# A decode layer's result as two rows of 320 in two PSUM banks, where it was four rows of 160 in one

## The chip, the cores and the metric

One core of one Trainium2 chip runs the kernel. The metric is the device time of one execution in microseconds (us), as the median of several runs. The engines are named as in the profile: PE is TensorE's matmuls, PEld its weight loads, DVE is VectorE, ACT is ScalarE, POOL is GpSimd, SP is SyncE, which here only issues transfers (DMA).

## The reference

One token (a row x of 640 values, bf16) goes through one layer: attention over a cache of 4096 positions with 32 heads, then a gated feed-forward part. Each part has a layer norm ahead of it and a residual sum behind it.

```
h   = x + attention(layernorm(x), K, V, wq) @ wo
n   = layernorm(h)
out = h + (gelu(n @ w_gate) * (n @ w_up)) @ w_down      # w_down: 1728 x 640
```

The change touches only the last line: the sum of h and the down projection, and how its 640 values leave PSUM.

## The kernel before, in words

The kernel is written instruction by instruction. `Prog` keeps one list for each engine in the order in which the program names the operations; each operation names those it waits for, and semaphores are made from that. An engine works through its own list in order, so an instruction that waits holds up all that is behind it on its engine. All large transfers are issued by SP, in one queue.

K and V of four heads at a time (4 MB) come into three slots in turn. For K, VectorE multiplies by the query (L273), TensorE sums by matmuls with the identity (L281), VectorE reduces (L288) and ScalarE takes the exponential (L292). For V, TensorE multiplies (L310). The query projection ahead of this (L259) is worked in sets of four matmuls of 512 columns, one on each quarter of the output partitions (from 0, 32, 64 and 96), with the sets alternating between PSUM banks 3 and 7. VectorE and ScalarE copy the two banks (L263, L264).

The end of the kernel, in TensorE's order:

- `proj_part` (L348) multiplies by wo. VectorE adds x (L404), which gives h with its values spread over partitions (`hT`, 128 x 5). Then come the layer norm and `hX` (L407), a 128 x 640 tile with each value of h on the diagonal.
- `glu(ps_g, ...)` (L417): the gate projection, 70 matmuls of one output column each.
- `resid` (L424 to L428): matmuls of a column of ones with `hX` put the values of h as a row on one partition in PSUM. They begin the accumulation (`start=True`) onto which the down projection adds. Both operands are fp32.
- `glu(ps_u, ...)` (L430, L431): the up projection, 70 more matmuls of line L417, in two parts, as its weights come in two transfers.
- VectorE and ScalarE work out the gelu of the gate (L432 to L439) beside this. L440 multiplies by the up projection: `hm`, 128 x 14 in bf16, one column for each block m of 128 rows of w_down.
- `hp` and `h2` (L451, L453) prepare the last, half-filled block (m = 13) so that its 64 rows lie over all 128 partitions.
- `down` (L442 to L450): for each block m, a matmul with one column of `hm` as the stationary operand and 640 columns of w_down as the moving one, in pieces. The order of the blocks follows the transfers: 12, then 0 to 3, 13, 4 to 7, 8 to 10, and 11 last, with a wait for the transfer ahead of each group. Block 11 has an operation of its own for each piece, so that each copy waits for its own piece.
- The copies (L460 on VectorE, L462 on ScalarE) bring the pieces from PSUM into `out_row` (1 x 640, bf16); SP then issues the output transfer.

Before the change a block has four pieces of 160 columns. They go to the partitions 0, 32, 64 and 96 of bank 3 (`ps_d`, L151), VectorE copies the first two and ScalarE the last two:

```
ps_d = bank[3][:, 256:416]
i = e.matmul(ps_d[32 * q:32 * q + 1, 0:160], h, wd_sb[:, m, n:n + 160],
             start=False, stop=(m == 11))
```

Bank 7, which the change uses as well, holds half of the query projection and later the wo projection (`ps_p`), which L404 has read by then.

Of the kernel before, what the change touches and what calls it, by code (L numbers as in the profile page):

```python
# [101 lines left out]
def bass_sequential_preLN__gqa_block_cached__glu_gated_geglu__decode_kernel(nc, A_x, A_k_cache, A_v_cache, A_wq, A_wo, B_x, B_w_gate, B_w_up, B_w_down, out):  # L102
# [11 lines left out]
    out_row = sb("out_row", [1, D], BF16)  # L114
# [4 lines left out]
    hX = sb("hX", [128, 128, 5], FP32)  # L119
# [13 lines left out]
    hm = sb("hm", [128, 14], BF16)  # L133
    hm2 = sb("hm2", [128, 2], BF16)
# [4 lines left out]
    ones_f = sb("ones_f", [128, 128], FP32)  # L139
# [6 lines left out]
    bank = [nc.alloc_psum_tensor("bank%d" % i, [128, 512], FP32) for i in range(8)]  # L146
# [1 line left out]
    ps_g, ps_u = bank[0], bank[1]  # L148
    ps_q = [bank[3], bank[7]]
    ps_a = bank[3]  # L150
    ps_d = bank[3][:, 256:416]  # L151
    ps_o = [bank[2], bank[4]]
    ps_s = bank[5]
    ps_z = bank[6]
# [6 lines left out]
    V = lambda fn, *d: P.op("vector", fn, *d)  # L161
    A = lambda fn, *d: P.op("scalar", fn, *d)
    T = lambda fn, *d: P.op("tensor", fn, *d)
# [199 lines left out]
    for kind, G in order:  # L363
# [7 lines left out]
        if G == 4:  # L371
# [15 lines left out]
    wd_sb = sl[1][:, 0:14 * D].rearrange("p (m n) -> p m n", m=14)  # L387
# [3 lines left out]
    d_wd = [P.dma("sync", wd_sb[:, 12, :], B_w_down[1536:1664, :], free[1]),  # L391
            P.dma("sync", wd_sb[:, 13, 0:320], B_w_down[1664:1728, :].rearrange("f (s n) -> (f s) n", s=2))]
# [11 lines left out]
    h = V(lambda e: e.tensor_add(hT[:, 0:5], xx[:, 0:5], ps_p[:, 0:5]), pr)  # L404
# [17 lines left out]


    def resid(e):  # L424
        for q in range(4):
            i = e.matmul(ps_d[32 * q:32 * q + 1, 0:160], ones_f[:, 0:1],
                         hX[:, 32 * q:32 * q + 32, :].rearrange("p a c -> p (a c)"), start=True, stop=False)
        return i  # L428
    T(resid, hx)
    T(glu(ps_u, wu_sb, range(3)), d_wu[0])  # L430
    up = T(glu(ps_u, wu_sb, range(3, 5)), d_wu[1])  # L431
# [7 lines left out]
    g6 = V(lambda e: e.tensor_mul(gu[:, :], g_t[:, :], t1[:, :]), g8)  # L439
    g9 = V(lambda e: e.tensor_mul(hm[:, :], gu[:, :], ps_u[:, 0:14]), g6, up)  # L440

    def down(ms, qs=range(4)):  # L442
        def fn(e):
            for m in ms:
                for q in qs:
                    h, n = (hm[:, m:m + 1], 160 * q) if m < 13 else (hm2[:, q // 2:q // 2 + 1], 160 * (q % 2))
                    i = e.matmul(ps_d[32 * q:32 * q + 1, 0:160], h, wd_sb[:, m, n:n + 160],  # L447
                                 start=False, stop=(m == 11))
            return i
        return fn  # L450
    hp = T(lambda e: e.matmul(ps_z[:, 0:1], sel2[:, :, :].rearrange("p a b -> p (a b)"), hm[0:64, 13:14],  # L451
                              start=True, stop=True), g9, c_sel2)
    h2 = V(lambda e: e.tensor_mul(hm2[:, :], par[:, :], ps_z[:, 0:1].to_broadcast([128, 2])), hp)  # L453
    T(down([12]), d_wd[0])
    T(down(range(4)), d_wd[2])
    T(down([13]), h2, d_wd[1])
    T(down(range(4, 8)), d_wd[3])
    T(down(range(8, 11)), d_wd[4])
    dn = {q: T(down([11], [q]), d_wd[5]) for q in (0, 2, 1, 3)}
    os = [V(lambda e, q=q: e.tensor_copy(out_row[0:1, 160 * q:160 * q + 160], ps_d[32 * q:32 * q + 1, 0:160]), dn[q])  # L460
          for q in range(2)]
    os += [A(lambda e, q=q: e.copy(out_row[0:1, 160 * q:160 * q + 160], ps_d[32 * q:32 * q + 1, 0:160]), dn[q])  # L462
           for q in range(2, 4)]
    d_out = P.dma("sync", out[0, :, :], out_row[:, :], *os)
    P.op("sync", None, d_out)

# [29 lines left out]
```

## Time and profile before

| what | value |
| --- | --- |
| time, median of 3 runs | 203.16 us (203.05 to 203.16) |
| profiled execution, span from the first to the last instruction (its whole time is not given apart) | 201.9 us |
| PE busy in the span | 120.4 us, 60% |
| DVE busy | 101.2 us, 50% |
| ACT busy | 61.1 us, 30% |
| read from HBM | 84.23 MB, 417 GB/s over the span |
| share of the chain that ended last: DMA, PE, DVE | 64%, 16%, 14% |
| mean granted TensorE clock, whole span | 0.825 |
| granted TensorE clock, from about 177 us on | 0.50 |
| L447 (down), PE | 56 matmuls of 128x160, mean 328 ns |
| L426 (resid), PE | 8 records of 128x160 fp32, mean 450 ns |
| L460 on DVE, L462 on ACT | 2 copies of 1x160 each, mean 314 and 286 ns |

How to read it: the profile is one execution, taken by the hardware. A busy share is an average over stages with different limits, so for a change at the end of the kernel the last microseconds are what counts: the chain of work that ended last, and the timeline from about 190 us on. In a timeline row stand the start, the length, the engine, the line, the operation with its output and input and how many there are; brackets give the idle time of the engine before it, and what ended it.

### The profile page before, as it was taken

The numbers are of one execution on the slowest core, as the hardware profiler recorded it, in microseconds if no ns is written. First come the engines' busy times: TensorE is split into PE (matmuls) and PEld (weight loads), VectorE is DVE, ScalarE is ACT, GpSimd is POOL, SyncE is SP. The second block draws the span as 40 slices with busy tenths as digits, with TensorE's granted clock in tenths as the row PEclk, the third lists the DMA queues.
The fourth block names the chain that finished last, engine by engine and source line by source line (L and its number), as shares of the span: only waits on it lengthen the run. The fifth ranks groups of instructions, "written<-read, shape, count | busy, mean of one in ns | idle before, by whom it ended". The sixth has DMA issues, their size and how long they took to land.

```text
span 201.9 us, 2505 instructions
## 1 busy us (share of the span) xinstructions
PE 120.4 (60%) x1010; PEld 58.8 (29%) x1010; DVE 101.2 (50%) x106; ACT 61.1 (30%) x273; POOL 5.0 (2%) x14
## 2 busy tenths in 40 slices
PE   0107058537937668690968197727844887467395
PEld 0103023112312233150324032312331344267383
DVE  3201088517979847924791578277708760100221
ACT  2101004620563550670156125603640363100101
POOL 7200000000000000000000000000000000000000
PEclk9999657995799996997599859988995799955555
DMA  9999999999999999999999999999999999999992
GB/s 357 414 404 467 428 415 416 422 448 458 430 415 422 415 445 448 435 424 416 422 435 441 438 435 424 416 428 441 448 419 435 399 425 437 419 408 435 412 409 113
DMA packets 4335, 84.39 MB, mean 418 GB/s; under 512 B 482, under 2 KB 868, under 8 KB 1508
## 3 DMA queue, kind: packets, MB, share of 16 engines
q1 hardware_dynamic: 4322, 84.23, 97.8%
q8 instruction: 8, 0.13, 0.3%
q14 instruction: 3, 0.02, 0.0%
q10 hardware_dynamic: 2, 0.00, 0.0%
HBM read 84.23 MB, written 0.00 MB: 417 GB/s over the span
## 4 chain that ended last, share of the span: by engine, by line
DMA 64%; PE 16%; DVE 14%; issue 3%; SPq 2%
DMA slot<-in_A_k_cache_dram 42%; DVE prod L273 12%; DMA slot<-in_B_w_down_dram 11%; DMA slot<-in_A_v_cache_dram 11%; PE bank L281 11%; PE bank L310 3%; SPq L51 2%; DVE sc L288 2%; PE bank L319 1%; PE bank L447 0%; DVE out_row L460 0%; PE bank L330 0%; DVE RT L329 0%
## 5 line engine op out<-in xcount | busy, mean ns | idle before, releaser
L281 PE MATMUL bank<-prod,id_b 128*128 128x512 bf16 x256 | 75.4, 454 | 50.8 <-DVE prod L273 50.8
L273 DVE TENSOR_TENSOR prod<-slot,qb 128x4096 bf16<-128x4096 bf16 x32 | 72.4, 2285 | 31.1 <-DMA slot<-in_A_k_cache_dram 31.1
L292 ACT ACTIVATE p_bd<-sc,zero_t 32x32 bf16<-32x32 f32 x128 | 46.4, 362 | 86.3 <-DVE sc L288 85.1
L281 PEld LDWEIGHTS bank<-prod,id_b 128*128 128x128 bf16 x256 | 26.9, 113 | 99.4 <-DVE prod L273 63.1
L288 DVE TENSOR_REDUCE sc<-bank 128x32 f32<-128x512 f32 x32 | 22.0, 688 | 21.4 <-PE bank L281 21.4
L292 ACT ACTIVATION_READ_ACCUMULATOR p_bd<-sc,zero_t 32x1 f32 x128 | 23.5, 184 | 0.0
L310 PE MATMUL bank<-slot,p_bd 128*16 128x512 bf16 x256 | 17.3, 379 | 3.1 <-ACT p_bd L292 2.5
L310 PEld LDWEIGHTS bank<-slot,p_bd 128*16 128x16 bf16 x256 | 9.4, 89 | 7.3 <-ACT p_bd L292 3.0
L319 PE MATMUL bank<-po_sb,hs 128*16 128x128 f32 x64 | 8.4, 274 | 1.1 <-ACT po_sb L314 1.1
L348 PE MATMUL bank<-aP,arena 128*128 128x1 bf16 x160 | 6.7, 178 | 3.8 <-DMA arena<-in_A_wo_dram 3.8
L417 PE MATMUL bank<-hlnT,slot 128*128 128x1 bf16 (+1 forms) x140 | 6.7, 176 | 3.2 <-DMA slot<-in_B_w_gate_dram 3.2
L259 PE MATMUL bank<-arena,xlnB 128*32 128x512 bf16 x40 | 3.9, 565 | 7.2 <-DMA arena<-in_A_wq_dram 7.2
L348 PEld LDWEIGHTS bank<-aP,arena 128*128 128x128 bf16 x160 | 6.6, 131 | 3.9 <-DMA arena<-in_A_wo_dram 2.5
L314 ACT COPY po_sb<-bank 128x512 f32<-128x512 f32 x8 | 4.7, 585 | 9.6 <-PE bank L310 9.6
L417 PEld LDWEIGHTS bank<-hlnT,slot 128*128 128x128 bf16 (+1 forms) x140 | 6.3, 118 | 4.1 <-DVE hX L407 3.3
L319 PEld LDWEIGHTS bank<-po_sb,hs 128*16 128x16 f32 x64 | 5.5, 96 | 4.5 <-issue 2.1
L244 ACT ACTIVATE ln<-ln,eps_t 128x1 f32<-128x1 f32 x2 | 0.6, 294 | 20.3 <-DVE ln L242 20.3
L263 DVE CAST qb<-bank 128x512 bf16<-128x512 f32 x1 | 0.7, 692 | 9.6 <-PE bank L259 9.6
L404 DVE TENSOR_TENSOR hT<-xx,bank 128x5 f32<-128x5 f32 x1 | 0.2, 163 | 10.2 <-PE bank L348 10.2
L233 PE MATMUL bank<-one_bf,x_row 1*128 1x1 bf16 x5 | 0.4, 177 | 6.9 <-DMA x_row<-in_A_x_dram 6.9
L259 PEld LDWEIGHTS bank<-arena,xlnB 128*32 128x32 bf16 x40 | 1.6, 136 | 9.1 <-issue 9.0
L334 DVE TENSOR_SCALAR aT<-bank,rz 16x128 bf16<-16x128 f32 x2 | 0.7, 339 | 6.0 <-PE bank L319 6.0
(65 smaller groups left out, 26.3 us busy)
## 6 DMA issues: line engine op xcount, KB each, us to landing
slot<-in_A_k_cache_dram SPq DMA_DIRECT2D x8, 4096.0 KB, 21.4
slot<-in_A_v_cache_dram SPq DMA_DIRECT2D x7, 4096.0 KB, 17.5
arena<-in_A_wq_dram SPq DMA_DIRECT2D x1, 5120.0 KB, 15.4
slot<-in_A_v_cache_dram SPq DMA_DIRECT2D x2, 2048.0 KB, 20.0
arena<-in_A_wo_dram SPq DMA_DIRECT2D x1, 2560.0 KB, 27.3
slot<-in_B_w_gate_dram SPq DMA_DIRECT2D x1, 2160.0 KB, 16.3
arena<-in_A_wo_dram SPq DMA_DIRECT2D x1, 1920.0 KB, 31.5
slot<-in_B_w_up_dram SPq DMA_DIRECT2D x1, 1296.0 KB, 18.4
```

The lines of the kernel that those rows point to most:

```text
L51: ev = self.op(eng, lambda e: e.dma_start(out, in_), *deps, dma=True)
L259: i = e.matmul(ps_q[hf][32 * j:32 * j + 32, :], xlnB[:, c, :], wq_j[:, c, j, 4 * hf:4 * hf + 4, :], start=(c == 0), stop=(c == 4))
L263: qa = V(lambda e: e.tensor_copy(qb[:, 0:4, :].rearrange("p g d -> p (g d)"), ps_q[0][:, :]), qd)
L273: m = V(lambda e: e.tensor_tensor(out=prod[:, s % 4, :, :], in0=kt[:, 32 * u:32 * u + 32, :], in1=qb[:, G, :].unsqueeze(1).to_broadcast([1 ...
L281: i = e.matmul(ps_f[s % 2][:, :], id_b[:, :], prod[:, s % 4, :, 16 * b:16 * b + 16], start=(b == 0), stop=(b == 7))
L288: reds[s] = V(lambda e: e.reduce_sum(sc[:, s % 4, :], ps_f[s % 2][:, :].rearrange("p (g d) -> p g d", d=16), axis=AX.X), folds[s], exps.ge ...
L292: x = A(lambda e, j=j: e.activation(p_bd[32 * j:32 * j + 32, G % 2, 32 * (s % 4):32 * (s % 4) + 32, j], sc[32 * j:32 * j + 32, s % 4, :], ...
L310: i = e.matmul(po[a:a + 16, :], p_bd[:, G % 2, 4 * b:4 * b + 4, :].rearrange("p g j -> p (g j)"), vt[:, 4 * b:4 * b + 4, :], start=(b < 4) ...
L314: evs[G] = A(lambda e: e.copy(po_sb[:, G % 2, :], po[:, :]), pvs[G], hds.get(G - 2))
L319: i = e.matmul(ps_a[0:16, 128 * (G // 4):128 * (G // 4) + 128], hs[:, r, 12 - 4 * g:28 - 4 * g], po_sb[:, G % 2, 128 * r:128 * r + 128], s ...
L348: r = e.matmul(ps_p[:, c:c + 1], wo_sb[:, t, i, c::5], aP[:, t, i:i + 1], start=(t == 0 and c == 0 and i == 0), stop=(t == 1 and i == 15), ...
L417: i = e.matmul(ps[0:128 if m < 13 else 64, m:m + 1], ws, hlnT[:, c:c + 1], start=(c == 0 and m == 0), stop=(c == 4), skip_group_check=True)
```

## The change

The result is kept as two rows of 320 instead of four of 160: one on partition 0 of bank 3, one on partition 32 of bank 7. The residual becomes two matmuls of 320 columns, the down projection 28 of 320 where it was 56 of 160. Each engine makes one copy of 320 where it made two of 160. Nothing else is changed: the transfers, the order of the blocks and the waits of TensorE stay.

```diff
-    ps_d = bank[3][:, 256:416]
+    ps_d = [bank[3][0:1, 0:320], bank[7][32:33, 0:320]]
...
     def resid(e):
-        for q in range(4):
-            i = e.matmul(ps_d[32 * q:32 * q + 1, 0:160], ones_f[:, 0:1],
-                         hX[:, 32 * q:32 * q + 32, :].rearrange("p a c -> p (a c)"), start=True, stop=False)
+        for q in range(2):
+            i = e.matmul(ps_d[q], ones_f[:, 0:1], hX[:, 64 * q:64 * q + 64, :].rearrange("p a c -> p (a c)"),
+                         start=True, stop=False)
         return i
...
-    def down(ms, qs=range(4)):
+    def down(ms, qs=range(2)):
         def fn(e):
             for m in ms:
                 for q in qs:
-                    h, n = (hm[:, m:m + 1], 160 * q) if m < 13 else (hm2[:, q // 2:q // 2 + 1], 160 * (q % 2))
-                    i = e.matmul(ps_d[32 * q:32 * q + 1, 0:160], h, wd_sb[:, m, n:n + 160],
-                                 start=False, stop=(m == 11))
+                    h, n = (hm[:, m:m + 1], 320 * q) if m < 13 else (hm2[:, q:q + 1], 0)
+                    i = e.matmul(ps_d[q], h, wd_sb[:, m, n:n + 320], start=False, stop=(m == 11))
             return i
...
-    dn = {q: T(down([11], [q]), d_wd[5]) for q in (0, 2, 1, 3)}
-    os = [V(lambda e, q=q: e.tensor_copy(out_row[0:1, 160 * q:160 * q + 160], ps_d[32 * q:32 * q + 1, 0:160]), dn[q])
-          for q in range(2)]
-    os += [A(lambda e, q=q: e.copy(out_row[0:1, 160 * q:160 * q + 160], ps_d[32 * q:32 * q + 1, 0:160]), dn[q])
-           for q in range(2, 4)]
+    dn = [T(down([11], [q]), d_wd[5]) for q in range(2)]
+    os = [V(lambda e: e.tensor_copy(out_row[0:1, 0:320], ps_d[0]), dn[0]),
+          A(lambda e: e.copy(out_row[0:1, 320:640], ps_d[1]), dn[1])]
```

## The prediction

> **What bounds the kernel now.** I read the page's chain of work first, then the chain from 150 us on, piece by piece, because the change touches only the end of the kernel. Its last pieces are:
>
> ```profile
> 176.80 22.42 DMA slot<-in_B_w_down_dram
> 199.22 0.04 issue
> 199.27 0.75 PE bank L447 x16
> 200.02 0.30 DVE out_row L460
> 200.32 0.03 issue
> 200.35 0.32 DVE out_row L460
> ```
>
> The columns are start, length and what it is. Up to 199.22 us the end is set by the weights of the down projection landing. Behind that stand only 0.75 us of matmuls and two copies of VectorE. Second, the timeline of the last 9 us shows what happens beside that transfer (start, length, what; in brackets the idle time before, and what ended it):
>
> ```profile
> 193.12 0.71 PE L426 MATMUL bank<-hX,ones_f 128*1 128x160 f32 x8
> ...
> 193.77 3.36 PE L417 MATMUL bank<-hlnT,slot 128*128 128x1 bf16 x70
> ...
> 197.24 0.17 DVE L440 TENSOR_TENSOR hm<-gu,bank 128x14 bf16<-128x14 f32 x1 [2.17 <-PE bank L417]
> ...
> 197.57 1.50 PE L447 MATMUL bank<-slot,hm 128*1 128x160 bf16 x40
> ...
> 199.27 0.71 PE L447 MATMUL bank<-slot,hm 128*1 128x160 bf16 x16 [0.19 <-DMA slot<-in_B_w_down_dram]
> 199.67 0.09 PEld L447 LDWEIGHTS bank<-slot,hm 128*1 128x1 bf16 x4 [0.18 <-DMA slot<-in_B_w_down_dram]
> 200.01 0.66 DVE L460 CAST out_row<-bank 1x160 bf16<-1x160 f32 x2 [2.17 <-PE bank L447]
> 200.04 0.59 ACT L462 CAST out_row<-bank 1x160 bf16<-1x160 f32 x2 [5.67 <-PE bank L447]
> 200.72 0.31 SPq L51 DMA_DIRECT2D out_dram<-out_row  x1
> ```
>
> What to see: from 193.12 on TensorE works through one queue almost without a gap: the residual (L426), the up projection (L417), ten rows of the down projection (forty matmuls, L447). Then it waits a moment for the last two transfers. So the transfer is the bound by a small margin, and TensorE is right behind it. The margin: a lone L447 matmul lasts 290 ns (the shortest in the view of line L447). With 160 columns at 0.83 ns (below) that is 0.13 us of streaming and 0.16 us until it is done. The forty are therefore streamed by 197.57 + 1.50 - 0.16 = 198.91, and the next could start 0.36 us before it does at 199.27.
>
> **What one matmul costs TensorE.** Line L447 has 56 matmuls of 328 ns on average, 18 us if they ran in turn; they are done in 1.50 + 0.71 us, so four run side by side, one on each quarter of the output partitions (0, 32, 64, 96). Ten fours take 1.50 - 0.16 = 1.34 us, 0.134 us for a four of 160 columns, or 0.83 ns per column. The query projection gives the same rate with other shapes. Its fours have 512 columns and alternate between banks 3 and 7, and their weight loads come every 0.43 us, again 0.83 ns per column (the page prints a clock near full for those first slices, but the spacing is that of the halved clock, twice what L281 has at 1.0, see rival A):
>
> ```profile
> 16.80 0.18 PEld L259 LDWEIGHTS bank<-arena,xlnB 128*32 128x32 bf16 x4 [0.24 <-issue]
> 17.22 0.18 PEld L259 LDWEIGHTS bank<-arena,xlnB 128*32 128x32 bf16 x4 [0.24 <-issue]
> 17.65 0.18 PEld L259 LDWEIGHTS bank<-arena,xlnB 128*32 128x32 bf16 x4 [0.24 <-issue]
> ```
>
> So a set of matmuls side by side costs the columns of one of them, however many lie beside it. That decides the case. The change halves the number of matmuls but doubles the columns of each, and only two quarters are in use instead of four. A row m of the down projection, now one set of 160 columns (0.133 us), becomes one set of 320 (0.267 us).
>
> **The sum, part by part.**
>
> 1. The residual (L426). The view shows eight records for four matmuls: an fp32 matmul passes twice, at 0.27 us a pass. It streams for 0.71 - 0.16 = 0.55 us. Two side by side with 320 columns need twice that: +0.53 us. It hides behind nothing: it stands in TensorE's queue ahead of the up projection, whose weights have landed (the view of transfers gives 20.0 us for the later part, issued at 174.91, so 194.9; it is needed about 195.8), and hm (L440) waits for the up projection, while the gate's part of it is ready at 195.06 (L439). So hm and all behind it slip by 0.53: the first L447 starts at 198.10.
> 2. The down projection. Fourteen sets of 0.267 are 3.73 us, and 0.16 until the last is done: 198.10 + 3.73 + 0.16 = 201.99. The last two transfers (waits ended at 199.27 and 199.67) are in by the time TensorE needs rows 8 and 11, at 200.77 and 201.57, so these waits go; what is late in their place is TensorE itself. Now its last matmul ends at 199.27 + 0.71 = 199.98: +2.01 us. Half the LDWEIGHTS (28 for 56) save nothing, as they lie beside the matmuls.
> 3. The copies. VectorE starts 0.03 after TensorE's end, ScalarE 0.06. Each now copies 160 elements twice, 0.66 and 0.59 us. No row has 320 in one partition, so by the rows on either side: VectorE takes 314 ns for 160 (L460) and 692 for 512 (L263), 1.07 ns more per element, so 314 + 172 = 486; ScalarE 286 (L462) and 585 (L264), so 286 + 136 = 422. The bounds are 314 (length costs nothing) and 632 (nothing but length). I take 486, as 1x160 lies on the same line as 128x14 (173 ns, L432). VectorE ends at 202.02 + 0.49 = 202.51, ScalarE at 202.05 + 0.42 = 202.47; now the end is 200.67. So the copies give back 0.17, and the end moves by +1.84. That the rows lie in two banks gains nothing that I can see: both engines read bank 3 at once today and both first and second copies take the same time (311 to 316, 285 to 286 ns).
> 4. The output transfer (L51) and the end of the program follow the later copy, as now. No transfer ahead of it is moved, and no queue but TensorE's gets longer work.
>
> Span 201.9 + 1.84 = 203.7. The profiled execution's own time is not given apart; the runs' median lies 1.26 above its span, and I add the difference to the median: 203.16 + 1.84 = **205.0 us**. About 0.2% (0.4 us) is what a measurement of this kernel can tell from no change.
>
> **Rivals.**
>
> *A, not slower: the clock opens in time.* The granted clock is 0.50 in every stretch from 177 us to the end. At 1.0 a column costs half: L281's eight matmuls of 512 take 1.90 us, less 0.16, which is 0.42 ns per column. Then a pair of 320 streams in 0.133 us, as a four does now; residual and ten rows end as before, TensorE waits for the transfers again, and what is left is the copies' -0.17: 203.0 us. To come out within 0.4 us of before, TensorE may slip by 0.58 us instead of 2.01, so 1.43 must be saved; as an open clock halves what is left to stream, it must open by 201.83 - 2.86 = 198.97. Against it speaks the view of windows, cut into stretches of 3.41 us, by which the clock's changes are spaced (length, TensorE busy, count, clock):
>
> ```profile
> 28.98:32.39 3.41, 3.41 (x9) 0.50 1.02 442
> 46.04:49.46 3.42, 2.53 (x6) 0.50 1.05 450
> ...
> 192.82:196.23 3.41, 3.41 (x72) 0.50 1.02 412
> ```
>
> After the first, full of 512-column matmuls, the clock was 1.0; after the second, filled to 74%, it was not; nor after the third, which is full, but mostly of 1-column matmuls. A stretch that ends by 198.97 would be nearly all L417. The Trainium skill, "TensorE: Matmul & The Clock Gate", section "What's actually happening", has the clock open after one busy window of some 3.4 us; by that rule, TensorE being in work from 189.85 on, the clock would be open well before the down projection and the result this rival's 203.0. The trace does not agree: 0.50 after a window that was 3.41 of 3.41 busy. Chance 3%.
>
> *B, the clock opens late.* A stretch that is over 75% full of L447 (74% was too little above) ends no earlier than 200.7. In the profile's phase the stretches end at 199.65 and 203.06, so none does; if the phase varies, one of them may fall between 200.7 and 201.8 and save half of what is left, up to 0.6 us: 204.4 to 204.95. A row of one column may also not count as work at all. Chance 12%.
>
> *C, the two rows do not run side by side*, because they lie in different banks. Then the residual streams 2.13 us (+1.6) and the down projection 28 x 0.267 = 7.47: the end of TensorE is 199.17 + 7.47 + 0.16 = 206.80, +6.82, less 0.17: 209.8 us. The fours of L259 keep their pace across a change of bank at each step, which speaks against it, though inside a four they share one. Chance 5%.
>
> **How the numbers follow.** The forecast has 80% (A 3, B 12, C 5). Its own spread is the copies' bounds (-0.17, +0.15) and some tenths for the slack between TensorE and the landings: 204.7 to 205.4. With B the range is 204.4 to 205.4. Slower by over 0.2%: forecast, B and C, 0.96 (1 point off for what I do not see); within 0.2%: A, 0.03; faster: 0.01.
>
> **What would show it.** Right: L447 x28 in one unbroken run of about 3.9 us, no wait for B_w_down before L447, L426 about 1.24 us long, the chain's end on PE L447 and the residual instead of the transfer, copies of about 0.49 and 0.42 us side by side. Wrong: a run of about 7.6 us (C), a granted clock above 0.50 after 193 us (A, B), or a wait for the transfer that is still the last.

## The result and the profile after

The changed kernel takes 204.99 us (median of 4 runs, 204.79 to 205.21) against 203.11 us for the kernel before on the same chip (4 runs, 203.01 to 203.16): a ratio of 1.0084, with a 95% interval of 1.0063 to 1.0105. The forecast was 205.0. The profiled execution took 205.21 us, with a span of 203.9 us, 2.0 us longer than the profiled span before. In the profiled executions of two experiments below (one_quarter, clock_open) the gate's weights came 2.2 to 2.4 us later than in the others; of these two profiles only lengths are used, not where they end, and one_quarter's profiled execution (210.82 us, a slow run) is left out of its ratio.

The chain of work that ended last, from the gate projection on (start, length, what):

```profile
174.42 15.49 DMA slot<-in_B_w_gate_dram
189.91 0.14 issue
190.05 3.35 PE bank L417 x70
193.39 1.16 PE bank L426 x4
194.56 3.31 PE bank L417 x70
...
198.37 3.87 PE bank L447 x28
202.24 0.47 DVE out_row L459
```

The transfer that the chain hangs on is now that of the gate's weights, which landed at 189.91; before, it was the down projection's, which landed at 199.22. From 190.05 on every step but the last copy is TensorE, or the short hop over VectorE for hm. The weights of the down projection, on which the chain hung before, are gone from it. The timeline of the same stretch:

```profile
193.32 1.23 PE L426 MATMUL bank<-hX,ones_f 128*1 128x320 f32 x4
...
194.49 3.37 PE L417 MATMUL bank<-hlnT,slot 128*128 128x1 bf16 x70
...
198.30 3.90 PE L447 MATMUL bank<-slot,hm 128*1 128x320 bf16 x28
...
202.23 0.48 DVE L459 CAST out_row<-bank 1x320 bf16<-1x320 f32 x1 [3.67 <-PE bank L447]
202.26 0.42 ACT L460 CAST out_row<-bank 1x320 bf16<-1x320 f32 x1 [7.69 <-PE bank L447]
202.77 0.31 SPq L51 DMA_DIRECT2D out_dram<-out_row  x1
```

L447 has no bracket any more: nothing stands between its first and its last matmul but TensorE itself. Half as many matmuls take 3.90 us, where the fifty-six took 1.50 + 0.71. The residual (L426) grew from 0.71 to 1.23 us. Each copy is one of 0.48 or 0.42 us, where two took 0.66 and 0.59. The gate projection began at 190.05, 0.20 us later than in the profile before; in the repetition below it began at 189.80, so that part belongs to the execution and not to the change.

### The profile page after: what moved, and what is told of

The parts are those of the page before. It is cut to its first block, busy times and chain, and to the rows that moved or that the text cites. A ratio compares the mean times of both kernels' runs of the same rounds, so it can differ in the third digit from the quotient of the medians.

```text
span 203.9 us, 2439 instructions
## 1 busy us (share of the span) xinstructions
PE 122.9 (60%) x978; PEld 58.8 (29%) x978; DVE 101.0 (50%) x105; ACT 60.9 (30%) x272; POOL 5.0 (2%) x14
## 4 chain that ended last, share of the span: by engine, by line
DMA 60%; PE 21%; DVE 14%; issue 2%; SPq 1%; DVEq 0%
DMA slot<-in_A_k_cache_dram 41%; DVE prod L273 12%; DMA slot<-in_A_v_cache_dram 11%; PE bank L281 11%; DMA slot<-in_B_w_gate_dram 8%; PE bank L310 3%; PE bank L417 3%; PE bank L447 2%; DVE sc L288 2%; PE bank L319 1%; SPq L51 1%; PE bank L426 1%; DVE out_row L459 0%; PE bank L330 0%; PE bank L450 0%
## 5 line engine op out<-in xcount | busy, mean ns | idle before, releaser
L310 PE MATMUL bank<-slot,p_bd 128*16 128x512 bf16 x256 | 18.1, 394 | 3.1 <-ACT p_bd L292 2.5
L259 PE MATMUL bank<-arena,xlnB 128*32 128x512 bf16 x40 | 3.7, 540 | 6.8 <-DMA arena<-in_A_wq_dram 6.8
L259 PEld LDWEIGHTS bank<-arena,xlnB 128*32 128x32 bf16 x40 | 1.5, 129 | 8.7 <-issue 8.5
L447 PE MATMUL bank<-slot,hm 128*1 128x320 bf16 x28 | 3.9, 468 | 0.0
```

The source lines that it names most:

```text
L259: i = e.matmul(ps_q[hf][32 * j:32 * j + 32, :], xlnB[:, c, :], wq_j[:, c, j, 4 * hf:4 * hf + 4, :], start=(c == 0), stop=(c == 4))
L310: i = e.matmul(po[a:a + 16, :], p_bd[:, G % 2, 4 * b:4 * b + 4, :].rearrange("p g j -> p (g j)"), vt[:, 4 * b:4 * b + 4, :], start=(b < 4) ...
L447: i = e.matmul(ps_d[q], h, wd_sb[:, m, n:n + 320], start=False, stop=(m == 11))
```

## The experiments

The theory: matmuls that write to different quarters of the output partitions lie side by side, and such a set costs the columns of one of them (0.83 ns each at the clock of this stage). The change makes TensorE's work longer by some 2.4 us (0.53 in the residual, 14 x 0.133 in the down projection). That is more than its slack behind the transfers, and TensorE takes the end from them. The rivals are that the banks, the number of matmuls, or the copies decide.

**after_again**: the changed kernel unaltered.

> The changed kernel unaltered, as the measure for the others of this set. Both theories: 205.0 us, 204.7 to 205.3.

Measured: 204.89 us (204.86 to 205.07), ratio 1.0090 (1.0073 to 1.0107). The span is 203.6 us; L426 takes 1.23 us and L447 3.85, 0.05 less than in the profile above: the granted clock opened shortly before its end (a timeline row, then TensorE in two windows: window, its length, busy time and count, granted clock, DMA share, GB/s):

```profile
198.04 3.85 PE L447 MATMUL bank<-slot,hm 128*1 128x320 bf16 x28
```

```profile
198.04:201.70 3.66, 3.66 (x29) 0.50 0.12 46
201.70:202.40 0.70, 0.19 (x2) 0.99 0.00 0
```

**one_quarter**: both rows on the same quarter, in different banks.

```diff
-    ps_d = [bank[3][0:1, 0:320], bank[7][32:33, 0:320]]
+    ps_d = [bank[3][0:1, 0:320], bank[7][0:1, 0:320]]
```

> Both rows on partition 0, in banks 3 and 7, so that no two matmuls can lie side by side. Theory of the columns: L426 about 2.3 us instead of 1.2, L447 28 x 0.267 + 0.16 = 7.6 us instead of 3.9, together +4.8: 209.8 us. Rival of the count (the time goes with the number of matmuls and not with where they are written): unchanged, 205.0 us.

Measured: ratio 1.0235 (1.0204 to 1.0265), some 207.9 us (207.22 to 208.43 in three runs). The timeline, and TensorE in two windows:

```profile
195.29 2.29 PE L426 MATMUL bank<-hX,ones_f 128*1 128x320 f32 x4
...
201.33 6.54 PE L447 MATMUL bank<-slot,hm 128*1 128x320 bf16 x28
```

```profile
204.70:206.40 1.70, 1.70 (x8) 0.50 0.00 0
206.40:208.00 1.60, 1.47 (x10) 0.94 0.00 0
```

The same 28 matmuls of the same shape, with the same two banks, take 6.54 us where they took 3.9, only because they share a quarter. The rival of the count falls. L426 meets its 2.3 us. L447 is 1.1 us short of the 7.6 expected, and the second window shows why: the granted clock rose during the run. From the start of the gate projection (192.01) to the issue of the output transfer (208.41) it is 16.40 us, 3.68 more than the 12.72 of the changed kernel: the 4.8 expected, less these 1.1.

**one_bank**: both rows in one bank, on different quarters.

```diff
-    ps_d = [bank[3][0:1, 0:320], bank[7][32:33, 0:320]]
+    ps_d = [bank[3][0:1, 0:320], bank[3][32:33, 0:320]]
```

> Both rows of 320 in bank 3, on partitions 0 and 32. Theory of the columns (matmuls on different quarters lie side by side, and a set costs the columns of one of them, 0.83 ns each, wherever the rows lie): unchanged, 205.0 us, L447 28 matmuls in 3.9 us, copies of 479 and 416 ns. Rival of the banks (that the rows lie in two banks costs the time): back towards 203.1 us; or, if the second bank spares the copies a wait, slower than 205.0 by the copies' growth.

Measured: 204.86 us (204.80 to 204.92), ratio 1.0086 (1.0071 to 1.0101). L447 takes as long as with two banks:

```profile
198.02 3.90 PE L447 MATMUL bank<-slot,hm 128*1 128x320 bf16 x28
```

The copies, now both from bank 3 at the same time, take 478 and 418 ns. The second bank neither costs nor gains anything.

**four_rows_two_banks**: the kernel before, with its four rows in two banks.

```diff
-    ps_d = bank[3][:, 256:416]
+    ps_d = [bank[3 if q < 2 else 7][32 * q:32 * q + 1, 256:416] for q in range(4)]
...
```

The lines left out use `ps_d[q]` in the residual, the down projection and the copies.

> The kernel before with its four rows of 160 spread over two banks: partitions 0 and 32 in bank 3, 64 and 96 in bank 7. VectorE reads bank 3 alone, ScalarE bank 7 alone. Theory of the columns: same as before, 203.1 us, fours still 0.133 us apart. Rival of the banks as a cost: towards 205.0. Rival of the banks as a gain (the two engines disturb each other in one bank): copies shorter than 311 to 316 and 285 to 286 ns, up to 0.2 us faster.

Measured: 203.08 us against 203.14, ratio 1.0002 (0.9969 to 1.0034). The first forty matmuls of L447 take as long as before:

```profile
197.49 1.50 PE L447 MATMUL bank<-slot,hm 128*1 128x160 bf16 x40
```

The copies take 313 to 316 and 285 to 287 ns. So of the change's two halves, other banks and fewer quarters, the first does nothing in either kernel.

**resid_early**: the changed kernel with `T(resid, hx)` ahead of `ga = T(glu(ps_g, ...))`.

> The changed kernel with the residual's two matmuls named ahead of the gate projection, where TensorE waits for the gate's weights. Theory (TensorE's own queue from the gate projection on sets the end, and the residual is 1.07 us of it): hX is there some 0.8 us before the gate's weights, so about 0.8 to 1.0 of the 1.07 us are hidden: 204.1 us, 203.9 to 204.4. Rival (the residual costs nothing, since the up projection has slack, and all of the loss is in the down projection): 205.0 us.

Measured: 204.20 us (median of 10), ratio 1.0055 (1.0031 to 1.0079), 0.7 us below after_again. The timeline:

```profile
189.07 1.23 PE L423 MATMUL bank<-hX,ones_f 128*1 128x320 f32 x4 [2.22 <-DVE hX L407]
190.23 6.67 PE L417 MATMUL bank<-hlnT,slot 128*128 128x1 bf16 x140
...
197.35 3.90 PE L447 MATMUL bank<-slot,hm 128*1 128x320 bf16 x28
```

Both projections run in one piece, and L447 begins 0.69 us earlier than in after_again (198.04). The residual was on the path. Less of it is hidden than expected (0.7 instead of 0.8 to 1.0): hX is ready 0.78 us before 189.80, where the gate began in after_again, but 0.05 us pass before the residual starts, and it then keeps the gate waiting until 190.23: the chain that ended last goes through the residual there, and not through the gate's weights.

**resid_twice**: the kernel before with the residual done twice.

```diff
-    def resid(e):
+    def resid(e, last=True):
...
+    T(lambda e: resid(e, False), hx)
     T(resid, hx)
```

> The kernel before with the residual's four matmuls done twice (the second time over the first result). It puts 0.55 us more into TensorE's queue ahead of the up projection. Theory (the last transfers set the end of the kernel before, and TensorE is 0.36 us behind them): 0.36 of it is hidden, and then all fourteen fours run in one piece: the end moves by about 0.17 us, 203.3 us, 203.15 to 203.45. Rival (TensorE sets the end already): 203.7. Rival (TensorE has a microsecond or more to spare): 203.1.

Measured: 203.62 us (median of 12), but the times scatter (203.10 to 205.88, ratio 1.0030, 0.9995 to 1.0065) and tell none of the three apart. The kernel before, run beside it, scatters as well (202.96 to 205.41); the cause is open. The trace does tell them apart:

```profile
193.09 1.25 PE L426 MATMUL bank<-hX,ones_f 128*1 128x160 f32 x16
...
198.10 2.04 PE L448 MATMUL bank<-slot,hm 128*1 128x160 bf16 x56
```

With 0.54 us more in its queue, TensorE is just the later one: the fourteen fours run in one piece of 2.04 us without a wait for the weights (the line is one further down in this kernel). They end at 200.14, 0.16 us later than before (199.98), though the gate began 0.04 us earlier. So in these two executions TensorE had about 0.35 us to spare behind the transfers (0.54 - 0.16 - 0.04).

**clock_open**: the changed kernel with 20 matmuls of 512 columns, whose result nobody reads, between the up projection and the down projection.

```diff
     up = T(glu(ps_u, wu_sb, range(3, 5)), d_wu[1])
+    fill(20)
...
```

`fill` is an added helper that names so many of these matmuls.

> The changed kernel with 20 matmuls of 128x512 with the identity, whose result nobody reads, between the up projection and the down projection. They are there to open TensorE's clock before the down projection, and cost 5 to 8.5 us themselves. Theory of the columns: with the granted clock at 1.0 the 28 matmuls of L447 run at half the time, 14 x 0.133 + 0.16 = 2.0 us instead of 3.9. Rival (a fixed cost for each matmul or a limit of the second operand's reading sets their pace): they stay above 3 us.

Measured once: 211.34 us, of which the fillers take 5.82 (one of their 20 records is missing); only the lengths within the trace are of use. The timeline, then windows:

```profile
200.34 5.82 PE L365 MATMUL bank<-prod,id_b 128*128 128x512 bf16 x19 [0.33 <-issue]
...
206.19 2.07 PE L455 MATMUL bank<-slot,hm 128*1 128x320 bf16 x28
```

```profile
200.30:203.50 3.20, 3.17 (x8) 0.50 0.03 12
206.00:208.30 2.30, 2.26 (x30) 1.00 0.00 0
```

The same 28 matmuls (here line L455) take 2.07 us at a granted clock of 1.0, where 2.0 were expected. Their pace goes with the clock, and a fixed cost that would hold them above 3 us is not there.

**clock_kept**: the changed kernel with 29 such matmuls in TensorE's own waiting times from 172 us on.

> The changed kernel with 29 such matmuls in the places where TensorE waits from 172 us on: 3 and 2 around the last sum of heads, 11 ahead of the first part of the wo projection, 6 ahead of its second, 7 ahead of the gate projection. If the clock, once open, stays open through the matmuls of one column, rival A of the prediction comes true: residual and down projection at half the time, and the time falls to about 203.0 to 203.5 us. If matmuls of one column do not keep it open, it is back at 0.50 during the gate or the up projection, and the time stays at 205.0, or some tenths above, should the fillers delay the gate projection.

Measured: 205.68 us (204.76 to 206.94), ratio 1.0109 (1.0075 to 1.0143). TensorE by windows:

```profile
177.50:181.00 3.50, 3.50 (x82) 1.00 0.98 415
...
182.50:186.00 3.50, 3.33 (x80) 0.98 1.05 429
186.00:190.00 4.00, 3.49 (x13) 0.50 0.97 412
190.00:193.20 3.20, 3.20 (x72) 0.50 0.99 416
```

The fillers held the clock open through the first part of the wo projection (the first row). It closed at the end of the second part, after a stretch of almost nothing but matmuls of one column (80 in the second row), and the seven fillers ahead of the gate (2.77 us) did not open it again. In the profiled execution the gate began at 189.85 and L447 took 3.90 us, as without fillers. What makes the times of this kernel scatter by 2 us is open.

**one_copy**: the kernel before with one VectorE copy for all four rows.

```diff
-    out_row = sb("out_row", [1, D], BF16)
+    out_row = sb("out_row", [128, 160], BF16)
...
+    os = [V(lambda e: e.tensor_copy(out_row[0:97, :], ps_d[0:97, 0:160]), *dn.values())]
+    d_out = P.dma("sync", out[0, 0, :].rearrange("(q n) -> q n", q=4), out_row[0:97:32, :], *os)
```

> The kernel before, with one VectorE copy of 97 partitions x 160 into a tile of the same shape instead of two copies of 1x160 on each of two engines; the output transfer then takes four pieces of 160 from partitions 0, 32, 64 and 96. Theory (a copy costs its columns, not its partitions): one copy of about 314 ns instead of 0.66 us, all that is saved being on the path behind the last matmul: -0.34 us, 202.8 us, 202.6 to 203.0. Rival (the output transfer of four pieces costs what the copy saves): 203.1.

Measured: 203.36 us against 203.14, ratio 1.0007 (0.9976 to 1.0038). The end of the timeline:

```profile
199.07 0.70 PE L447 MATMUL bank<-slot,hm 128*1 128x160 bf16 x16 [0.17 <-DMA slot<-in_B_w_down_dram]
...
199.90 0.33 DVE L460 CAST out_row<-bank 97x160 bf16<-97x160 f32 x1 [2.24 <-PE bank L447]
200.25 0.62 SPq L51 DMA_DIRECT2D out_dram<-out_row  x1
```

The copy of 97 partitions takes 0.33 us where two in turn took 0.66, as the theory says. The gain is spent at once. The copy waits for all four matmuls and starts 0.13 us after them (0.03 before), and issuing the transfer in four pieces takes SP 0.62 us instead of 0.31. From TensorE's end to the end of the span it is 201.9 - 199.77 = 2.1 us, against 201.9 - 199.98 = 1.9 before. Most of these 0.2 us pass behind the issue, and what they are is not shown. The rival holds: the transfer of four pieces costs at least what the copy saves.

**one_copy_resid_early**: the same, with the residual ahead of the gate.

> The same with the residual ahead of the gate projection, where TensorE waits. Theory (the last transfers set the end, so that TensorE's 0.55 us saved are worth nothing): as with one copy alone, 202.8 us. Rival (in most executions TensorE is the later one): up to 0.2 us faster than that.

Measured: 203.35 us (median of 12), ratio 0.9994 (0.9968 to 1.0020). The level expected (202.8) fails with one_copy; the question of whether TensorE's time is worth anything here is answered by the timeline:

```profile
196.78 0.97 PE L447 MATMUL bank<-slot,hm 128*1 128x160 bf16 x24
198.03 0.70 PE L447 MATMUL bank<-slot,hm 128*1 128x160 bf16 x16 [0.28 <-DMA slot<-in_B_w_down_dram]
199.17 0.70 PE L447 MATMUL bank<-slot,hm 128*1 128x160 bf16 x16 [0.44 <-DMA slot<-in_B_w_down_dram]
```

TensorE begins the down projection 0.6 us earlier than in one_copy (196.78 against 197.40) and waits for the weights all the same, before 198.03 and before 199.17: with four quarters, the transfers set the end. No version here beats the kernel before.

## Why the prediction was right

- **The step that decided the case**, that a set costs the columns of one matmul whatever lies beside it, held: fourteen sets in 3.90 us, less the 0.16 us after the last, are 0.267 us each, as put down. one_quarter and clock_open show the same from two other sides. The query projection (L259), the prediction's second support, bears it out too. Its weight loads come every 0.43 us up to 18.50, but the matmuls of its last two sets start only 0.21 us apart (18.84 and 19.05). That fits a clock that opened there, after sets at the halved one, though the profile prints 1.00 throughout.
- **The residual**: +0.53 predicted, 1.23 - 0.71 = +0.52 measured. That nothing hides it: L447 begins 8.25 us after the gate projection, 7.72 before (198.30 - 190.05, 197.57 - 189.85). resid_early shows the same, where moving the residual brings 0.7 us.
- **The slack** of TensorE behind the transfers: 0.36 us predicted; resid_twice shows about 0.35 by the trace. As the margin is this small, TensorE took over the end.
- **The copies**: 486 and 422 ns predicted, 479 and 416 measured. Two banks gain nothing: shown in both directions by one_bank and four_rows_two_banks.
- **The sum**: from the start of the gate projection to the issue of the output transfer it is 200.72 - 189.85 = 10.87 us before and 202.77 - 190.05 = 12.72 after: +1.85, predicted +1.84. The end of TensorE moves by 12.15 - 10.13 = +2.02 in it, predicted +2.01. That the median (204.99) meets the forecast (205.0) to 0.01 us is luck, as the four runs lie between 204.79 and 205.21.
- **Rival A** did not come. Its price for the down projection was right: at a clock of 1.0 the 28 matmuls take 2.07 us (its 203.0 us as a whole was never measured). What fails is its condition, an open clock: after the 80 one-column matmuls of the wo projection's second part it closed in clock_kept, and those of the gate and up projections ran at 0.50 without opening it.
- **Rival B** is real, and too late to matter. A granted clock above 0.50 after 193 us, which the prediction named as a sign of being wrong, did appear. The profile after, in stretches of 3.41 us:

```profile
192.16:195.57 3.41, 3.41 (x58) 0.50 1.01 413
195.57:198.99 3.42, 3.09 (x56) 0.50 0.77 304
198.99:202.40 3.41, 3.21 (x25) 0.50 0.01 5
202.40:203.90 1.50, 0.00 (x0) 0.99 0.00 1
```

After a stretch of L447 alone the clock opened at 202.40, 0.20 us after the last matmul. In after_again it opened at 201.7, some 0.2 us ahead of the end, and saved 0.05 us. In one_quarter the run was long enough, and the clock opened well within it. "TensorE: Matmul & The Clock Gate" of the Trainium skill, section "What's actually happening", lets one busy window open the clock. The trace agrees where the window is filled with streams of 320 columns (3.21 of 3.41 us busy), and disagrees where it is filled mostly with matmuls of one column (3.41 of 3.41 busy in the first row, clock still 0.50 in the second).

- **Rival C** (the rows do not lie side by side because of the banks) fell with the run of 3.90 us and with one_bank. Its price was too high by some 2 us when it was built as one_quarter: 209.8 predicted, about 207.9 measured. In the profiled execution the clock that opened in the middle is all that is missing (1.1 us); the other runs were not traced.

## What to carry to other kernels

Count TensorE's time in columns streamed by sets that lie side by side, not in matmuls: with one row of output, four pieces on four quarters take half the time of two pieces of double length on two. Before one saves instructions on an engine that is off the path, its slack is to be read off (here 0.36 us against 2.4 us added). A shorter copy is worth only what the steps behind it, the issue of the output transfer above all, do not take back.

## What was not expected of the hardware

- Issuing one output transfer of 1280 bytes took SP 0.31 us from one partition and 0.62 us from four (320 bytes each).
- The granted clock opened in stretches in which the matmuls wrote a single row of output (one_quarter: 6.54 us with one output row at a time), but not in a stretch that was 3.41 of 3.41 us busy, for the most part with matmuls of 128 rows of output and one column. So busy time, as the profile counts it, is not enough to open it.
- The 80 one-column matmuls of each part of the wo projection take the same time at either clock: 3.36 and 3.33 us at 0.50 in the kernel before, 3.36 and 3.33 us at 1.00 in clock_kept. The gate and up projections, with matmuls of the same shape, were not run at 1.00.
